# Attention and feed-forward on one core: two turned pairs of heads in one visit of TensorE, their last 64 query rows as float32 products in quarters of the array

## The chip, the cores and the metric

One Trainium2 chip, one core of it. The metric is the device time of one execution in microseconds (us), the median of several runs. The engines are named as in the profile: PE (TensorE, matrix products), PEld (its weight loads), DVE (VectorE), ACT (ScalarE), POOL (GpSimd), SP (SyncE, which issues most DMA transfers).

## The reference, cut to what matters

```python
B, H, S, D = 8, 8, 576, 64                # q, k, v: (B, H, S, D); f: (B, H, S)
scores = q @ k.T / sqrt(D)                # per batch and head
cum = cumsum(log(clip(f, 1e-4, 1)))
scores = where(above the diagonal, -1e9, scores + cum[:, None] - cum[None, :])
attn = softmax(scores)                    # rows, less their maximum
x = (attn @ v), heads side by side        # (4608, 512)
h = x @ w_in                              # (4608, 2048)
g = max(h, 0) + alpha * min(h, 0)
out = g @ w_out                           # (4608, 512)
```

Inputs and outputs are float32 (the two weight matrices arrive as float64 words and are rebuilt on the chip).

## The kernel before, in words

The work is 32 pairs of heads (n = 0 to 31, four pairs a batch), then a first feed-forward product in 9 blocks of 512 tokens (`ffn1(b)`, 192 products of 128x128 by 128x512 each), then a second one in 18 units of 256 tokens (`ffn2(u)`). The order is not written out: every operation is handed to a planner (`Plan.run`) with an engine, an estimated duration, a key and the buffers that it needs, and the planner puts each engine's operations in a fixed order. The key is a due time plus a number from the table `SHIFT` (one for each step letter and pair). An operation with `glue` may be chosen although PE would have to wait for it up to that many us; `need=(ring, k)` holds an operation back until k buffers of a ring are free or their last readers have been placed. Engines then run their lists in order, and wait on semaphores where data or buffers are late.

PSUM has 8 banks, shared by rings: `rS` (scores, tails and, from batch 1 on, the values' results), `rH` (blocks of `ffn1`, two banks are kept for it), `rT` (transposes).

Pairs 8 to 31 are "turned": their rows of attention are transposed by DVE and DMA, not by PE. For a turned pair n, `attention(n)` makes these steps:

- `load_n`: q and k of both heads (one tile `rqk`, two of them) come in; ACT and POOL split them into high and low float32r parts Qh, Ql, Kh, Kl (ring `rQ`, two sets); tile 0's q and k are copied as they are to a small tile `qk`, since the first 128 query rows are done as one float32 product. The decay goes to Z (128 by 2 by 1280, ring `rZ`, two) and Zt.
- `visit`: PE makes, in one go, the values of an earlier pair (`values`, products of 128 rows by 64 columns, both heads side by side) and then the scores of this pair: tiles 0 and 1 in one bank for each head, tile 2, tile 3; six banks. Each score is three float32r products (Qh Kh, Qh Kl, Ql Kh); the two heads lie in the two halves of the array's rows (64 by 128).
- `tail`: the last 64 query rows of both heads as one product of 128 by 128. For this the host lays q out with blocks of zeros (640 columns in place of 576). Three float32r products for 256 and three for 320 key columns, in two banks. The planner puts them anywhere after the visit, or before it.
- `tile` and `red` in `tail`: DVE takes each bank, adds the decay, finds the row's minimum (L830, L680) and writes to `bE`, a single buffer of 3136 columns for a whole pair; ACT takes the exponential in place (`expo`, L637). When all nine parts are done, DVE transposes `bE` in four pieces (L846) and 16 DMA transfers lay them out for `values`. Until then the next turned pair can't write to `bE`, and its banks stay full.
- `quotients` and `rest`: the sums' reciprocals go through DRAM; `rest` scales the values' result and splits it for `ffn1`, into a ring `rx` of seven buffers, of which a block of `ffn1` holds four until its last product.

`ffn1` fills the time between the visits, in pieces of six products. Each of its banks is emptied by ACT (L1027) and then DVE (L1029).

Of the kernel before, what the change touches and what calls it, by code (L numbers as in the profile page):

```python
# [18 lines left out]
NP = H // 2  # L19
# [25 lines left out]
LAG = 2000  # L45
PJ = (2, 4, 6)
# [8 lines left out]
SHIFT = {('L', 0): 9.4, ('D', 0): 2.2, ('Z', 0): 60.6, ('A', 0): 2.2, ('T', 0): -0.3, ('V', 0): -13.3, ('Q', 0): 36.2, ('X', 0): -10.8, ('L', 1): 26.8, ('D', 1): 1.4, ('Z', 1): -27.5, ('A', 1): 47.1, ('T', 1): 17.0, ('V', 1): 48.8, ('X', 1): 122.0, ('L', 2): 28.7, ('D', 2): 45.5, ('Z', 2): 10.6, ('A', 2): 54.0, ('T', 2): 1.8, ('V', 2): 58.1, ('Q', 2): -44.8, ('X', 2): 24.9, ('L', 3): 15.8, ('D', 3): -69.7, ('Z', 3): 0.9, ('A', 3): 165.1, ('T', 3): -84.7, ('Q', 3): 0.7, ('D', 4): -10.7, ('Z', 4): 63.2, ('A', 4): 13.0, ('T', 4): 4.2, ('V', 3): 35.9, ('Q', 4): 132.1, ('X', 3): -15.3, ('L', 5): 81.7, ('D', 5): -4.2, ('Z', 5): -0.4, ('A', 5): 21.2, ('T', 5): -65.7, ('V', 4): 1.3, ('Q', 5): -3.4, ('X', 4): 18.4, ('L', 6): 69.8, ('D', 6): 30.4, ('A', 6): 173.3, ('T', 6): 64.2, ('V', 5): 16.9, ('L', 7): 15.0, ('D', 7): -6.8, ('Z', 7): -95.9, ('A', 7): 218.4, ('T', 7): 47.3, ('V', 6): -17.7, ('V', 7): -37.7, ('Q', 7): -7.0, ('X', 5): -14.8, ('X', 6): -7.2, ('W', 0): 14.3, ('W', 1): 178.8, ('W', 2): 130.1, ('W', 3): -7.0, ('W', 4): 29.0, ('W', 5): 13.1, ('W', 6): 131.9, ('W', 7): -0.1, ('W', 8): -24.7, ('W', 9): 48.7, ('W', 10): -21.0, ('W', 11): -226.7, ('W', 12): -27.8, ('W', 13): 9.3, ('W', 14): 110.8, ('W', 15): 19.8, ('L', 8): -132.0, ('D', 8): -70.2, ('Z', 8): -11.8, ('S', 8): 10.0, ('A', 8): 59.0, ('L', 9): 6.4, ('D', 9): -6.1, ('Z', 9): 32.3, ('S', 9): -81.3, ('A', 9): -1.9, ('Q', 9): -96.4, ('X', 7): 3.1, ('L', 10): 50.1, ('Z', 10): 7.2, ('S', 10): 75.8, ('A', 10): -14.4, ('V', 8): -29.5, ('L', 11): 6.9, ('Z', 11): 41.4, ('S', 11): -6.8, ('A', 11): -68.7, ('V', 9): 12.9, ('Q', 11): 10.9, ('X', 8): 37.3, ('X', 9): 119.6, ('L', 12): 6.3, ('Z', 12): -18.6, ('S', 12): 23.7, ('A', 12): -9.9, ('V', 10): -2.9, ('L', 13): 2.6, ('Z', 13): -3.7, ('S', 13): 27.4, ('A', 13): 27.1, ('V', 11): -0.8, ('Q', 13): -134.7, ('X', 10): 5.7, ('X', 11): 5.8, ('L', 14): 1.6, ('Z', 14): 459.3, ('S', 14): -32.6, ('A', 14): -10.4, ('V', 12): 1.0, ('L', 15): 34.3, ('Z', 15): 17.4, ('S', 15): 96.4, ('A', 15): -40.5, ('V', 13): -69.9, ('Q', 15): -38.3, ('X', 13): 4.3, ('L', 16): 2.7, ('Z', 16): -198.9, ('S', 16): -187.7, ('A', 16): 154.9, ('V', 14): -18.6, ('L', 17): -9.2, ('Z', 17): 0.6, ('S', 17): 49.4, ('A', 17): -109.5, ('Q', 17): -229.2, ('X', 14): 26.2, ('X', 15): -29.2, ('L', 18): -40.0, ('Z', 18): -30.3, ('S', 18): 19.5, ('A', 18): -44.4, ('V', 16): 8.7, ('L', 19): -4.1, ('Z', 19): 16.8, ('S', 19): -29.0, ('A', 19): -99.9, ('V', 17): -19.8, ('Q', 19): -113.9, ('X', 16): 4.8, ('X', 17): -2.5, ('L', 20): -18.2, ('Z', 20): -4.1, ('S', 20): 3.5, ('A', 20): -15.6, ('V', 18): -13.2, ('L', 21): 24.2, ('Z', 21): -5.1, ('S', 21): 30.9, ('A', 21): 1.5, ('V', 19): -12.3, ('Q', 21): -6.5, ('X', 18): -66.7, ('X', 19): 21.5, ('L', 22): -197.2, ('Z', 22): -25.6, ('S', 22): -118.4, ('A', 22): 52.2, ('V', 20): 46.3, ('L', 23): 3.6, ('Z', 23): 49.0, ('S', 23): 3.0, ('A', 23): -4.3, ('V', 21): 106.1, ('Q', 23): -43.7, ('X', 20): 27.7, ('X', 21): -18.4, ('L', 24): -6.9, ('Z', 24): 91.0, ('S', 24): 17.4, ('A', 24): 103.3, ('V', 22): -23.4, ('L', 25): -7.9, ('Z', 25): 14.7, ('S', 25): -51.9, ('A', 25): 20.7, ('V', 23): 21.8, ('Q', 25): 14.2, ('X', 22): 35.9, ('X', 23): -3.3, ('L', 26): -42.8, ('Z', 26): 29.2, ('S', 26): 11.4, ('A', 26): 78.5, ('V', 24): 156.6, ('L', 27): -38.3, ('Z', 27): 1.9, ('S', 27): 40.9, ('A', 27): 0.5, ('Q', 27): 2.0, ('X', 24): -6.8, ('X', 25): 12.5, ('L', 28): -1.5, ('Z', 28): -21.7, ('S', 28): 28.1, ('A', 28): -23.8, ('V', 26): 13.8, ('L', 29): 6.3, ('Z', 29): -5.4, ('S', 29): -109.1, ('A', 29): -4.1, ('V', 27): -32.8, ('Q', 29): -0.6, ('X', 26): -3.0, ('X', 27): -14.3, ('L', 30): -20.4, ('Z', 30): 3.6, ('S', 30): 13.5, ('A', 30): 40.4, ('V', 28): 9.6, ('L', 31): -7.6, ('Z', 31): -99.0, ('S', 31): 13.9, ('A', 31): -1.5, ('V', 29): 16.7, ('V', 31): 16.3, ('V', 30): -2.0, ('Q', 31): -48.0, ('X', 28): -51.3, ('X', 29): -14.3, ('X', 30): -12.2, ('X', 31): -79.3}  # L55
# [167 lines left out]
def attention_moe(  # L223
# [54 lines left out]
    def split_set(i):  # L278
        return (sp.tile([128, QW - 128], F32R, name=f"Qh{i}"), sp.tile([128, QW - 128], F32R, name=f"Ql{i}"),
                sp.tile([128, S], F32R, name=f"Kh{i}"), sp.tile([128, S], F32R, name=f"Kl{i}"), sp.tile([128, 256], F32, name=f"qk0{i}"))  # L280
# [3 lines left out]
    rqk = Ring(Store(qkt))  # L284
    rZ = Ring(Store([(sp.tile([128, 2, ZW], F32, name=f"Z{i}"), sp.tile([128, S], F32, name=f"Zt{i}")) for i in range(2)]))
# [198 lines left out]
    def load_n(n, held):  # L484
# [5 lines left out]
        q_, k_ = (lambda: bqk.t[:, 0:QW]), (lambda: bqk.t[:, QW : QW + S])  # L490
# [3 lines left out]
        if n < NQ:  # L494
            l_qk = [op("SP", 450, lambda c0=c0, c1=c1: sy.dma_start(bqk.t[:, c0:c1], qk[p][:, c0:c1]), kq, dq, [bqk], kb=(c1 - c0) / 2)
                    for c0, c1 in ((0, QW), (QW, QW + S))]
        else:
            l_qk = [op("SP", 500, lambda: sy.dma_start(bqk.t[:, 0:1024].rearrange("p (c n) -> p c n", c=2), qk1[b, p].rearrange("c p n -> p c n")), kq, dq, [bqk], kb=400),
                    op("SP", 500, lambda: sy.dma_start(bqk.t[:, 1024:], qk2[b, p]), kq, dq, [bqk], kb=96)]
# [74 lines left out]
        else:  # L574
            tz = [op("SP", 400, lambda h=h, c8_=c8_: sy.dma_start(Zt()[64 * h : 64 * h + 64], c8_[bh + h : bh + h + 1].broadcast_to([64, S])), kl + 1, o_, [bZ], kb=147) for h in range(2)]
# [9 lines left out]
        q0, k0_ = (lambda: bQ.t[4][:, 0:128]), (lambda: bQ.t[4][:, 128:256])  # L585
        out += [op("ACT", c_acs(128), lambda: ac.activation(q0(), q_()[:, 0:128], AF.Copy), kc, l_qk[:1], [bqk, bQ]),
# [12 lines left out]

    waiting, behind, later_x, quick_ops, value_ops, turn_ops = [], [], [], [], [], []  # L600

    def attention(n):

        b, p = divmod(n, NP)
        k0 = NS * n
# [788 lines left out]
```

## Time and profile before

| | |
|---|---|
| median of 3 runs | 990.89 us (990.79 to 997.57) |
| the profiled execution: time, span of the core | 990.63 us, 988.8 us |
| PE busy, PEld busy | 982.2 us (99%), 827.5 us (84%) |
| DVE, ACT, POOL busy | 830.7 us (84%), 614.4 us (62%), 375.5 us (38%) |
| granted TensorE clock | 1.000 over the span |
| transferred | 191.68 MB, 194 GB/s mean |

An engine's busy time is the union of its instructions' spans. PE's instructions overlap, so what one costs is read from the starts of the instructions after it, not from its own length.

### The profile page before, as it was taken

To read this page: it belongs to the slowest core of one execution; us is meant where nothing else is said; L and a number is where in the kernel's file an instruction comes from. 1 tells how busy PE (TensorE), PEld (TensorE's weight loads), DVE (VectorE), ACT (ScalarE), POOL (GpSimd) and SP (SyncE) were. 2 spreads that over 40 slices of the span, in tenths; PEclk is the share of its full clock that TensorE was granted. 3 is DMA by queue.
4 is the path that set the end of the run, shared out by engine and by line. 5 is a ranking of instruction groups with operands and counts; after the bars stand their busy time and mean duration, and the time that the engine had idled before them with its cause. 6 is when DMAs were issued, how large, how long until landed. Compare 5 with 4: busy or idle time off the path is not lost.

```text
span 988.8 us, 20133 instructions
## 1 busy us (share of the span) xinstructions
PE 982.2 (99%) x6935; PEld 827.5 (84%) x6935; DVE 830.7 (84%) x1585; ACT 614.4 (62%) x1399; POOL 375.5 (38%) x652
## 2 busy tenths in 40 slices
PE   9999999999999999999999999999999999999998
PEld 5777788888888888888888888999888988898898
DVE  6899988878787778779637988789999999999995
ACT  7888887878677686767635655645444543544352
POOL 5465976888868797777350000000000000000000
PEclk9999999999999999999999999999999999999999
DMA  7977768888888798796757655553444344334521
GB/s 216 260 215 259 251 217 247 254 246 262 247 251 255 224 261 249 219 267 200 215 180 237 203 172 200 174 170 107 149 128 149 107 149 155 122 107 149 169 67 43
DMA packets 133876, 191.68 MB, mean 194 GB/s; under 512 B 22647, under 2 KB 84590, under 8 KB 133774
## 3 DMA queue, kind: packets, MB, share of 16 engines
q1 hardware_dynamic: 128878, 175.73, 57.2%
q0 software_dynamic: 4608, 14.46, 5.3%
q8 instruction: 55, 0.90, 0.4%
q14 instruction: 47, 0.39, 0.1%
q10 hardware_dynamic: 288, 0.20, 0.1%
HBM read 102.95 MB, written 48.67 MB: 153 GB/s over the span
## 4 chain that ended last, share of the span: by engine, by line
PE 96%; DVE 2%; issue 1%; DMA 0%; ACT 0%; DVEq 0%; ACTq 0%
PE bank L381 93%; PE bank L651 2%; PE bank L444 0%; DMA wr<-in_w_in_dram 0%; DVE xs L939 0%; DVE hs L371 0%; DVE big L830 0%; PE bank L729 0%; PE bank L479 0%; DVE hs L1316 0%; DVE big L646 0%; DVE hs L368 0%; DVE wr L371 0%; DVE hs L367 0%; DVE wr L368 0%
## 5 line engine op out<-in xcount | busy, mean ns | idle before, releaser
L381 PE MATMUL bank<-xx,wi 128*128 128x512 f32 x1728 | 407.2, 392 | 0.0
L381 PEld LDWEIGHTS bank<-xx,wi 128*128 128x128 f32 x1728 | 320.4, 188 | 69.6 <-issue 3.0
L637 ACT ACTIVATE big<-big,st 128x384 f32<-128x384 f32 (+4 forms) x272 | 157.7, 582 | 25.8 <-DVE st L830 24.2
L1029 DVE SCALAR_TENSOR_TENSOR hs<-bank,sa,hs 128x512 f32<-128x512 f32 x116 | 86.5, 745 | 54.0 <-ACT hs L1027 52.5
L1027 ACT ACTIVATE hs<-bank,ab 128x512 f32<-128x512 f32 x116 | 79.7, 687 | 70.6 <-PE bank L381 69.0
L830 DVE CUSTOM_DVE_ANT_0 big<-bank,Z 128x384 f32<-128x384 f32 (+1 forms) x220 | 93.0, 480 | 34.2 <-PE bank L381 27.7
L1268 ACT ACTIVATE xx<-gj 128x1792 fp32r<-128x1792 f32 x37 | 62.4, 1701 | 95.0 <-DVE gj L1261 57.3
L381 PE MATMUL bank<-wot,xx 128*128 128x256 f32 (+1 forms) x734 | 120.6, 323 | 0.0
L381 PE MATMUL bank<-wi,xx 128*128 128x256 f32 (+1 forms) x734 | 120.6, 323 | 0.0
L381 PEld LDWEIGHTS bank<-wi,xx 128*128 128x128 f32 x734 | 106.8, 189 | 12.2
L381 PEld LDWEIGHTS bank<-wot,xx 128*128 128x128 f32 x734 | 106.8, 189 | 12.2
L846 DVE STREAM_TRANSPOSE big<-big 128x768 f32<-128x768 f32 x96 | 90.3, 959 | 8.5 <-ACT big L637 8.5
L543 POOL TENSOR_TENSOR Z<-Z,tri 128x128 f32<-128x128 f32 x192 | 79.8, 444 | 34.3 <-DVE Z L513 30.7
L1269 DVE TENSOR_TENSOR xx<-gj,xx 128x1792 fp32r<-128x1792 f32 x37 | 74.4, 2018 | 2.5 <-ACT xx L1268 2.5
L943 POOL TENSOR_TENSOR xx<-xs,xx 128x256 fp32r<-128x256 f32 x64 | 49.0, 781 | 43.2 <-ACT xx L941 42.7
L381 PEld LDWEIGHTS bank<-big,vr 128*64 128x64 f32 x1168 | 53.7, 137 | 9.1 <-issue 5.5
L381 PE MATMUL bank<-wi,gh 128*128 128x256 f32 (+1 forms) x370 | 60.9, 322 | 0.0
L381 PE MATMUL bank<-wot,gh 128*128 128x256 f32 (+1 forms) x370 | 60.9, 322 | 0.0
L381 PE MATMUL bank<-big,vr 128*64 128x128 f32 (+1 forms) x1168 | 59.7, 260 | 0.0
L381 PEld LDWEIGHTS bank<-wot,gh 128*128 128x128 f32 x370 | 53.9, 189 | 6.0
L381 PEld LDWEIGHTS bank<-wi,gh 128*128 128x128 f32 x370 | 53.9, 189 | 6.0
L1298 ACT ACTIVATE hs<-bank 128x256 f32<-128x256 f32 x102 | 36.5, 384 | 24.9 <-PE bank L381 24.6
(164 smaller groups left out, 1585.6 us busy)
## 6 DMA issues: line engine op xcount, KB each, us to landing
hd<-hs SPq DMA_DIRECT2D x144, 256.0 KB
gj<-hd SPq DMA_DIRECT2D x50, 512.0 KB
rqk<-in_qk_dram SPq DMA_DIRECT2D x28, 512.0 KB
wx<-hd SPq DMA_DIRECT2D x22, 512.0 KB
vr<-in_vv_dram SPq DMA_DIRECT2D x32, 320.0 KB
wr<-in_w_in_dram SPq DMA_DIRECT2D x16, 512.0 KB
wx<-in_w_out_dram SPq DMA_DIRECT2D x16, 512.0 KB
out_dram<-hs SPq DMA_DIRECT2D x30, 256.0 KB
```

The costliest lines, as they stand in the source:

```text
L381: pe.matmul(o, lhsT, rhs, start=start, stop=stop)
L543: ms.append(op("POOL", c_po(128), lambda to=to, i=i, zd=zd: po.tensor_tensor(to()[:, :, -1:], zd()[:, :, i : i + 1], tk(), ALU.add), kc + ...
L637: ex = op("ACT", c_exp(w), lambda: ac.activation(at(bt.t), at(bt.t), AF.Exp, bias=lo()[:, col : col + 1], scale=-1.0, accum_out=su()[:, co ...
L651: pe.transpose(t[:, c : c + 128], src[:, 128 * j : 128 * j + 128], ident)
L830: ve.tensor_tensor_reduce(out=o if turned else blk(o), in0=blk(bS.t[:, c0 : c0 + w]), in1=in1(), scale=-0.125, scalar=3.0e38, op0=ALU.add, ...
L846: ve.transpose(part(b_[:, 0 : 768 if k < 3 else MW]), part(bE.t[:, c0 : c0 + (768 if k < 3 else MW)]))
L943: xl = op("POOL", c_po(256), lambda r=r, t0=t0: po.tensor_tensor(bx.t[:, 1, t0 : t0 + 256], bxs[r].t[:, 0:256], bx.t[:, 0, t0 : t0 + 256]. ...
L1027: cp = op("ACT", c_act(512), lambda bh=bh, bs=bs, fc=fc: ac.activation(bs.t, bh.t, AF.Relu, scale=ab[:, fc : fc + 1]), -1000, [last, o_sg] ...
L1029: cp = op("DVE", c_dve(512), lambda bh=bh, bs=bs, fc=fc: ve.scalar_tensor_tensor(bs.t, bh.t, sa[:, fc : fc + 1], bs.t, ALU.mult, ALU.add), ...
L1268: hi = op("ACT", c_acs(896 * GW), lambda w=w, bgh=bgh: ac.activation(bgh.t[:, 0], w(), AF.Copy), key, [o2], [bj, bgh])
L1269: lo = op("DVE", c_dve(896 * GW), lambda w=w, bgh=bgh: tt(bgh.t[:, 1], w(), bgh.t[:, 0].bitcast(F32), ALU.subtract), key + 0.1, [hi], [bj, ...
L1298: side = op("ACT", c_act(256), lambda m=m, slot=slot: ac.activation(bs.t[:, slot], bo[m].t[:, 256:512], AF.Copy), kd, [last], [bo[m], bs])
```

## The change

Turned pairs are taken two at a time by `couple(n)`: `attention` becomes a generator `steps` that stops after its loads and again after its scores.

- PE's visit for a couple is now: tails of both pairs against the first 256 keys, tails of both against the other 320 keys, scores of pair n, values of two earlier pairs, scores of pair n+1. All are keyed -3000 with glue 1.5; the first tail operation also needs five banks of `rS` (`NEED`).
- A tail is now one float32 product of 64 by 64 for each head, with no zeros: head h of pair n in row half h and column half h, of pair n+1 in row half h and column half 1-h (`swap`), so that the four products of a step lie in the four quarters of the array. The odd pair's tail rows therefore come out with the heads exchanged; its Zt, its sums' columns, its side of `bri` and its tail blocks in `values` are exchanged to match.
- The odd pair's tail can't go to `bE` yet; DVE writes it to a new tile `tt`, from where `expo` takes it to `bE`.
- Tile 0's float32 product and the tails read q and k from `rqk` itself: the two copies to `qk` are gone, Qh and Ql have 384 columns (512 before), and `rqk` is held until the pair's scores are done. For turned pairs q arrives with 576 columns (640 before).
- `later_x` keeps three pairs back (two before), and the whole table `SHIFT` is another.

```diff
-        for hi, lo, raw, z, w, ld in ((Qh, Ql, q_, 128, QW, l_qk[:1]), (Kh, Kl, k_, 0, S, l_qk)):
+        for hi, lo, raw, z, w, ld in ((Qh, Ql, q_, 128, 512, l_qk[:1]), (Kh, Kl, k_, 0, S, l_qk)):
...
-        held.append(bQ)
+        held += [bQ, bqk]
...
+    def couple(n):
+
+        pair = steps(n), steps(n + 1)
+        got = [next(g) for g in pair]
+        vals = [behind.pop(0) for _ in range(min(2, len(behind) - 1))]
+        go = sum([d() for _, d in vals], []) + got[0][0] + got[1][0]
+        for g, (c0, c1) in enumerate(TC):
+            plan.at("A", n)
+            bS = [Buf(rS) for _ in range(2)]
+
+            def tails(bS=bS, g=g):
+                for (_, _, quarter, _), b_ in zip(got, bS):
+                    quarter(g, b_.t)
+
+            s = op("PE", c_m4(c1 - c0) + (20 if g else 170), tails, -3000, go, bS + got[0][1] + got[1][1], glue=1.5, need=None if g else (rS, NEED))
+            for (_, _, _, lowest), b_ in zip(got, bS):
+                lowest(g, s, b_)
+            go = [s]
+        run = [pair[0].send(go)]
+        for f_, d in vals:
+            vb, vp, vd, done = f_()
+            run.append(op("PE", ns_v[0] + 400, vp, -3000, [run[-1]], vb, glue=1.5))
+            value_ops.append(run[-1])
+            done(run[-1])
+        pair[1].send([run[-1]])
...
+        def quarter(g, t):
+
+            q, k = terms[3]
+            for h in range(2):
+                r, o, (c0, c1) = slice(64 * h, 64 * h + 64), 64 * (h ^ swap), TC[g]
+                mm(t[o : o + 64, : c1 - c0], q(512, S)[r], k()[r, c0:c1], True, True)
+
+        def lowest(g, s, bS):
+
+            plan.at("A", n)
+            c0, c1 = TC[g]
+            low.append(op("DVE", c_dve(c1 - c0) + 60, lambda: ve.tensor_tensor_reduce(
+                out=aside.t[:, c0:c1] if swap else tail_at(bE.t)[:, c0 // 64 : c1 // 64], in0=cut(bS.t[:, : c1 - c0]), in1=cut(bZ.t[1][:, c0:c1]), scale=-0.125, scalar=lo()[:, 9:10] if g else 3.0e38,
+                op0=ALU.add, op1=ALU.min, accum_out=lo()[:, 4:5] if g else lo()[:, 9:10]), k0 - 1 + 0.6 * g, [s, rt] + low, [bS, aside if swap else bE, bst, bZ]))
...
-        def visit(st):
+        def visit(st, go):
 
             plan.at("A", n)
-            after = behind.pop(0) if len(behind) > 1 else None
-            go = rdy
-            if after:
-                vb, vp, vd, done = after()
-                a = op("PE", ns_v + 400, vp, st, rdy + vd, vb, need=(rS, len(vb[:2]) + 4))
-                value_ops.append(a)
-                done(a)
-                plan.at("A", n)
-                go = [a]
...
+        if turned:
+            where = visit(k0, (yield rdy, held, quarter, lowest))
+            yield s_0[-1]
+            plan.at("A", n)
...
-    for n in range(NX[0], B * NP):
-        attention(n)
+    for n in range(NX[0], B * NP, 2):
+        couple(n)
```

## Rows read from the trace of the kernel before

**Rows 1.** The chain that ended last, its final piece: start us, us, engine and line.

```profile
498.06 483.88 PE bank L381 x2864
```

**Rows 2.** Busy time by stretch: stretch and its length, then each engine, clock, DMA.

```profile
127.00:250.00 123.00, 123.00 (x997) 101.45 (x997) 100.89 (x253) 94.89 (x276) 99.83 (x183) 1.00 0.82 242
250.00:375.00 125.00, 125.00 (x1065) 104.42 (x1063) 98.37 (x247) 92.25 (x268) 100.11 (x178) 1.00 0.84 249
375.00:501.00 126.00, 126.00 (x1082) 104.74 (x1076) 96.71 (x246) 87.98 (x255) 84.96 (x152) 1.00 0.79 227
501.00:660.00 159.00, 159.00 (x845) 135.87 (x846) 121.92 (x180) 87.31 (x122) 8.19 (x13) 1.00 0.57 191
660.00:820.00 160.00, 160.00 (x979) 142.51 (x979) 152.71 (x191) 71.71 (x88) 0.00 (x0) 1.00 0.42 135
```

**Rows 3.** PE's timeline, 285 to 295 us: start us, us, then what ran, count.

```profile
285.27 0.39 PE L381 MATMUL bank<-Kh,Qh 128*128 128x256 f32 x1
285.49 0.28 PE L381 MATMUL bank<-Kl,Qh 128*128 128x256 f32 x1
285.61 0.28 PE L381 MATMUL bank<-Kh,Ql 128*128 128x256 f32 x1
...
286.17 8.35 PE L381 MATMUL bank<-xx,wi 128*128 128x512 f32 x36
294.45 0.33 PE L381 MATMUL bank<-wr,vr 128*64 128x128 f32 x2
```

**Rows 4.** PE's timeline, 323 to 334 us: one visit, and a tail later.

```profile
322.78 2.99 PE L381 MATMUL bank<-wr,vr 128*64 128x128 f32 x60
325.70 0.39 PE L381 MATMUL bank<-Kh,Qh 64*128 64x256 f32 x2
...
326.29 0.42 PE L381 MATMUL bank<-Kh,Qh 64*128 64x384 f32 x2
...
326.90 0.39 PE L381 MATMUL bank<-Kh,Qh 64*128 64x512 f32 x2
...
327.69 5.74 PE L381 MATMUL bank<-xx,wi 128*128 128x512 f32 x24
333.27 0.28 PE L381 MATMUL bank<-Kh,Qh 128*128 128x256 f32 x1
...
333.62 0.31 PE L381 MATMUL bank<-Kh,Qh 128*128 128x320 f32 x1
...
334.06 0.39 PE L381 MATMUL bank<-xx,wi 128*128 128x512 f32 x1
```

**Rows 5.** PE's timeline, 82 to 84 us: an early pair's tail, in float32.

```profile
82.65 0.60 PE L381 MATMUL bank<-rqk 128*128 128x256 f32 x2
83.09 0.49 PE L651 MATMUL bank<-ident,big 128*128 128x128 f32 x3
83.42 0.70 PE L381 MATMUL bank<-rqk 128*128 128x320 f32 x2
83.96 0.27 PE L729 MATMUL bank<-ident,st 128*9 128x128 f32 x1
```

**Rows 6.** DVE's timeline, 315 to 330 us: one pair's scores, tail and transposes.

```profile
315.29 0.29 DVE L830 CUSTOM_DVE_ANT_0 big<-bank,Z 128x128 f32<-128x128 f32 x1 [2.31 <-PE bank L381]
...
316.40 0.55 DVE L830 CUSTOM_DVE_ANT_0 big<-bank,Z 128x384 f32<-128x384 f32 x1
...
318.58 0.42 DVE L680 CUSTOM_DVE_ANT_0 big<-bank,Zt 128x256 f32<-128x256 f32 x1
...
319.18 0.55 DVE L680 CUSTOM_DVE_ANT_0 big<-bank,Zt,st 128x320 f32<-128x320 f32 x1 [0.17 <-DVE st L680]
...
320.89 0.75 DVE L1029 SCALAR_TENSOR_TENSOR hs<-bank,sa,hs 128x512 f32<-128x512 f32 x1
...
329.54 0.29 DVE L830 CUSTOM_DVE_ANT_0 big<-bank,Z 128x128 f32<-128x128 f32 x1 [0.17 <-DVE big L846]
```

**Rows 7.** Groups of 127 to 501 us, POOL: line, engine, operation, count, busy us, mean ns.

```profile
L595 POOL TENSOR_TENSOR Ql<-rqk,Qh 128x512 fp32r<-128x512 f32 x22 | 28.5, 1295 | 14.0 <-ACT Qh L590 13.7
```

**Rows 8.** The timelines of PE and of POOL around 212 us.

```profile
209.74 5.60 PE L381 MATMUL bank<-xx,wi 128*128 128x512 f32 x24
...
215.35 0.73 POOL L943 TENSOR_TENSOR xx<-xs,xx 128x256 fp32r<-128x256 f32 x1
```

More of the change, by code (lines that the diff above doesn't have):

```diff
@@ L489, in load_n @@
         bqk, bZ = Buf(rqk), Buf(rZ)
-        q_, k_ = (lambda: bqk.t[:, 0:QW]), (lambda: bqk.t[:, QW : QW + S])
+        late = n >= NX[0]
+        wq = S if late else QW
+        q_, k_ = (lambda: bqk.t[:, 0:wq]), (lambda: bqk.t[:, wq : wq + S])
+        side = n >= NX[0] and n % 2
         plan.at("L", n)
@@ L574, in load_n @@
         else:
[L575 removed]
+            tz = [op("SP", 400, lambda h=h, c8_=c8_: sy.dma_start(Zt()[64 * (h ^ side) : 64 * (h ^ side) + 64], c8_[bh + h : bh + h + 1].broadcast_to([64, S])), kl + 1, o_, [bZ], kb=147) for h in range(2)]
         plan.at("Z", n)
@@ L596, in load_n, with steps @@
                     lo()[:, a0 - z : a1 - z], raw()[:, a0:a1], hi()[:, a0 - z : a1 - z].bitcast(F32), ALU.subtract), kc, [o1], [bqk, bQ]))
-        held.append(bQ)
-        return out, rz, rt, bZ, [(lambda a, b, q=q: q()[:, a - 128 : b - 128], k) for q, k in ((Qh, Kh), (Qh, Kl), (Ql, Kh))] + [(lambda a, b: q0(), k0_)]
-    waiting, behind, later_x, quick_ops, value_ops, turn_ops = [], [], [], [], [], []
+        held += [bQ, bqk]
+        return out, rz, rt, bZ, [(lambda a, b, q=q: q()[:, a - 128 : b - 128], k) for q, k in ((Qh, Kh), (Qh, Kl), (Ql, Kh))] + [(lambda a, b: q_()[:, a:b], k_)]
+    waiting, behind, later_x, quick_ops, value_ops, turn_ops, ns_v = [], [], [], [], [], [], []
     def attention(n):
+        for _ in steps(n):
+            pass
+    def couple(n):
[20 more added lines that the diff above has]
+        pair[1].send([run[-1]])
+        for g in pair:
+            for _ in g:
+                pass
+    def steps(n):
         b, p = divmod(n, NP)
@@ L612, in attention @@
         turned = NX[0] <= n < NX[1]
+        swap = turned and n % 2
         plan.at("L", n)
@@ L665, in tail @@
             plan.at("A", n)
-            bt = bE if turned else Buf(re)
+            bt = Buf(re)
             prev = None
@@ L793, in stretch @@
             after = behind.pop() if tiles == (2,) and behind else None
-            vb, vp, vd, done = after() if after else ([], lambda: None, [], lambda o: None)
-            ns = 340 + sum(c_row(128 * i + 128, nt_) for i in tiles) + (ns_v if after else 0)
+            vb, vp, vd, done = after[0]() if after else ([], lambda: None, [], lambda o: None)
+            ns = 340 + sum(c_row(128 * i + 128, nt_) for i in tiles) + (ns_v[0] if after else 0)
             s = op("PE", ns, lambda: (prods(), vp()), st, rdy + vd, [x for y in bS for x in y] + held + vb)
@@ L951, in attention @@
         k_ = (0, 2, 6, 8) if n < NE else (0, 0.5, 2, 3) if turned else (0, 2, 8, 6)
-        bt = None
+        bt = where = None
+        if turned:
+            where = visit(k0, (yield rdy, held, quarter, lowest))
+            yield s_0[-1]
+            plan.at("A", n)
+        mate = waiting[-1] if n >= NV2 and n % 2 else None
+        bsu = mate[0] if mate else bst
+        if turned:
+            bt = bE
+            nt = expo(bE, S, 4, k0 - 0.4, low[1:], tail_at, (lambda: aside.t.rearrange("p (m c) -> p m c", c=64)) if swap else None, [aside] if swap else [])
         for tiles in ((0, 1), (2,), (3,)) if n < NE else ((2, 3, 0, 1),) if turned else ((0, 1, 3), (2,)):
-            where = visit(k0) if turned else stretch(tiles, -61 if n + tiles[0] == 0 else k0 + k_[tiles[0]])
+            where = where or stretch(tiles, -61 if n + tiles[0] == 0 else k0 + k_[tiles[0]])
             for i in tiles:
@@ L969, in values @@
                     lambda o: [done_v(r, bP[r])(o) for r in (1, 0)])
-        behind.append(values)
+        behind.append((values, v_deps))
         plan.at("V", n)
@@ L990, in attention @@
         elif not (n >= NV2 and n % 2 == 0):
-            keep = 2 if turned else 1
+            keep = 3 if n > NX[0] + 1 else 2 if turned else 1
             for f_ in later_x[:-keep]:
```

59 lines of the change are left out of this document (29 added, 30 removed).

## The prediction

> **What bounds the kernel now.** I read the chain of waits first. Its last piece is PE alone for 483.88 us [rows 1], and most of the chain before it is PE too. Then the busy time by stretch: PE is busy for all of 127 to 501 us, where the turned pairs run, and for all that follows up to 820 us, while POOL, DVE and ACT are busy for 67 to 82% of the first three stretches [rows 2]. So from 127 us on the time is the sum of PE's products. The timeline of PE must show whether that busy time has waits in it, since a busy PE may only be a full pipeline. It has nearly none: 36 products of `ffn1` take 8.28 us, 0.23 each, and the values after them start without a gap [rows 3]; the visits have one pattern throughout (values 2.92 us, scores 1.99, tail 0.80) [rows 4]. A us of PE taken out of this stretch comes off the end, if nothing else becomes late, and a us of waiting put in comes on top. Work saved on POOL, ACT or DMA is worth nothing by itself.
>
> **The sum, part by part.** It is made against the profiled execution, 990.63 us (span 988.8 and 1.83 around it); the median of the runs is 0.26 above it.
>
> *Tails removed.* Among products of `ffn1` a tail takes from 333.27 to 334.06 = 0.79 us, 0.35 for the step of 256 keys and 0.44 for that of 320 [rows 4]. There are 24 of them (a count over the timeline: 144 products, six a pair): 19.0 us.
>
> *Tails added.* The trace has no 64 by 64 product. What a float32 product costs by its columns is in the early pairs: two passes, 0.44 us for 256 columns and 0.54 for 320 [rows 5]. If the four quarters run at the same time, a couple costs 0.44 + 0.54 = 0.98, twelve couples 11.8 us. If they run two at a time it is 1.96 and 23.5 us, one by one 47 us. That is the disputed price. Nearest rows: the two heads of a score lie in halves of the rows, and three products of 512 columns for both take 0.79 us with the switch after them, where one such product of `ffn1` takes 0.23, so the heads overlap [rows 3, 4]. The two heads of the values lie in halves of the columns; 20 products of 128 and 10 of 64 columns would, at 0.11 us a pass by the 0.44 of 256 columns, take about 5.5 us in a row and take 2.92 [rows 4, 5], so they overlap too. Row halves and column halves each work, with different moving data in each; I take four at a time: saved 19.0 - 11.8 = 7.2 us.
>
> *Switches.* When the array goes from one division to another, the first product takes longer: 0.22 us in place of 0.12 for the tail right behind scores [rows 3], so about 0.10 a switch. Before, two pairs have six (into the values, into the scores, back to 128 by 128, twice); now there are five (tails, scores, values of two pairs together, scores, back). Saved 12 x 0.1 = 1.2 us.
>
> *Waits inside the longer visit.* This is the added cost, and nothing in the trace shows it, since before the values come first and give the banks time. Count from the first tail product, with six banks for the visit. PE: tails until 0.98, switch 0.1, scores of tiles 0 and 1 0.59, of tile 2 0.61, of tile 3 0.79 with the switch behind it [rows 4]; so tile 3 is reached at 2.3 and the values at 3.1 us. DVE: it starts some 0.3 after the first step's 0.44; the four tail parts take 0.35, 0.35, 0.48, 0.48 (a part is read from its start to the next one's, 0.61 for the widest), the four of tiles 0 and 1 together 1.11 (315.29 to 316.40) [rows 6]. So the tails' banks are free at 2.4 and those of tiles 0 and 1 at 3.5: a wait of 0.1 before tile 3 and 0.4 before the values, 0.5 a couple. It is less if a bank that `ffn1` has left is taken, or if a piece of `ffn1` is placed between (then two switches, 0.2); it is more if DVE has an `ffn1` bank to empty in between, 0.75 [rows 6]. Bounds 0 and 1.5 us a couple (two such banks); I take 0.3, near the count: +3.6 us.
>
> *Steps moved, at no cost.* The second pair's scores can't be emptied until the first pair's `bE` is transposed. Before it is the same: scores made from 325.70 were first read at 329.54 [rows 4, 6]. A pair holds `bE` for 14.3 us (315.29 to 329.54), a couple for 28.5, and a couple has 374/12 = 31 us; the cover is 2.7 us a couple, and if it goes, PE runs `ffn1` on two banks as it did then. The odd pair's tail goes through `tt` with the same DVE and ACT operations. POOL loses the copies to `qk` and a quarter of the Ql subtraction (0.3 of 1.3 us each [rows 7]), ACT as much: hidden work, worth nothing. `rqk` is held longer, so the next loads are issued later; behind them in SP's queue stand the stores of `ffn1` blocks and the layouts of `bE`. Loads and splits of a couple have the some 20 us between two visits. The first 127 us keep their operations; only the table reorders them: 0, with 3 us to either side. The second product follows PE and keeps its length.
>
> Sum: -7.2 - 1.2 + 3.6 = -4.8 us; 990.63 - 4.8 = 985.8, and 0.26 for the median: **986 us**.
>
> **Rivals.**
>
> *No waits and a better start.* If the banks are always free in time and the table takes 2 us out of the first 127: -8.4 - 2 = -10.4, **980.5**. For it: DVE is idle for a fifth of these stretches [rows 2], and before it hid every such wait. Against: the count above, with DVE at once on the tails, still gives 0.5.
>
> *Two quarters at a time.* 23.5 - 19.0 - 1.2 = +3.3; the slower tails give DVE time, so waits are 0 to 2 us more: **995**. For it: no row shows four. Against: both kinds of halves overlap in the rows above. The Trainium skill has a rule of this kind: TensorEngine Tiling (Array Packing), section Restrictions and Gotchas, says that different row tiles cannot access the same PSUM bank simultaneously, and here the two heads of one pair, in different row halves, write one bank. By that rule the heads of a pair would have to take turns, and the sum would be this one; no run here shows such a case, as the scores' heads have a bank each.
>
> *The visit waits for DVE (slower).* The place is the six banks between the tails and the values. If DVE is behind by two `ffn1` banks (2 x 0.75) when the tails come, each couple loses 1.5 us: -8.4 + 18 = +9.6, **1000**. It decides from 8.4/12 = 0.7 us a couple, not far above my 0.5. For it: DVE is 77 to 82% busy [rows 2], the tails are now first and in a burst, and nothing else on PE covers it once the visit has begun. Against: before, no visit shows a wait.
>
> *`ffn1` runs dry.* A block needs the values of four pairs. Values now come up to a pair later (those of pair 11 went with pair 13's visit, and go between the scores of 14 and 15). Before, block 2 began at 212.5 us, in the middle of the first of these rows, and the last piece of its input was written at 216.1 [rows 8], so there was nothing to spare; later blocks have more. One stall of up to 10 us, 5 taken: -4.8 + 5, **991**.
>
> **How the numbers follow.** Forecast (986, from 982 to 989.5 with waits of 0 to 0.6 a couple) 0.45; no waits 0.20; two at a time 0.10; DVE's waits 0.12; dry 0.13. The range holds the forecast, most of the better case, the dry one and two at a time, and leaves out the far half of the better case and DVE's: 979.5 to 997. Faster by over 1% means under 981.0, about what a measurement tells from no change: 0.14, from the better case. Slower by over 1%, over 1000.8: 0.07, half of DVE's case and quarters one by one. Within: 0.79.
>
> **What would show it.** In the trace after: 64 by 64 tail products that start four together and take about 1.0 us of PE a couple (two at a time: 2.0); DVE's tail parts running while PE is at the scores; a gap before the values of 0 to 0.5 us; PE's last turned stretch ending 5 us earlier, and the second product as long as before. I am wrong if the quarters wait for each other, if gaps in the visit exceed 0.7 us a couple, or if the first 127 us move by more than 3.

## The result, and the profile after

The changed kernel takes 1004.6 us (median of four runs, 1002.34 to 1010.89) beside 991.1 of the kernel before: ratio 1.0145, 95% interval 1.0117 to 1.0173. The forecast was 986.0, its range ended at 997. The profiled execution took 1002.34 us (span 1000.6, 11.8 longer than before).

**Where the loss lies.** The second product is as long as before. The chain's last piece now starts later and ends at 993.66 us, where it ended at 981.94 before [rows 1], and from the last product of `ffn1` to that end it is 350.1 us in both kernels. That last product (of block 8, where the turned stretch ends) starts at 643.56 us instead of 631.81, and the 126th product of `ffn1`, about where the turned pairs begin, at 118.81 instead of 117.69. So some 11 us are lost between 119 and 644 us.

```profile
515.24 478.42 PE bank L383 x2840
```

The windows that answer to [rows 2] show it: in the first three PE is no longer busy throughout, and there DVE, ACT and POOL are no busier than before, but for DVE in the first.

```profile
127.00:250.00 123.00, 120.03 (x957) 92.30 (x955) 103.23 (x270) 89.29 (x264) 88.22 (x162) 1.00 0.77 227
250.00:375.00 125.00, 123.87 (x990) 98.63 (x987) 90.41 (x220) 82.97 (x243) 90.09 (x163) 1.00 0.82 236
375.00:501.00 126.00, 122.90 (x1046) 97.01 (x1046) 88.66 (x226) 80.14 (x232) 78.79 (x141) 1.00 0.73 215
501.00:660.00 159.00, 159.00 (x906) 134.62 (x905) 121.25 (x193) 90.77 (x144) 19.71 (x29) 1.00 0.62 204
660.00:820.00 160.00, 160.00 (x998) 143.37 (x997) 152.76 (x192) 74.07 (x94) 0.00 (x0) 1.00 0.43 138
```

**The tails came out as forecast.** PE's timeline, the start of a visit (it answers to [rows 4]): the sixteen records of the quarters take from 177.91 to 179.04, 1.13 us with the switch into them. Eleven of the twelve visits have this length; one, at 412.59, takes 2.54, since `rqk` came late. A piece of six products of `ffn1` lies inside the visit, between two parts of a pair's scores; the last row is the values that follow.

```profile
177.12 0.86 PE L383 MATMUL bank<-xx,wi 128*128 128x512 f32 x3
177.91 1.20 PE L383 MATMUL bank<-rqk 64*64 64x256 f32 x16
179.04 0.39 PE L383 MATMUL bank<-Kh,Qh 64*128 64x256 f32 x2
...
179.82 1.65 PE L383 MATMUL bank<-xx,wi 128*128 128x512 f32 x6
181.40 0.45 PE L383 MATMUL bank<-Kh,Qh 64*128 64x384 f32 x2
...
182.83 1.42 PE L383 MATMUL bank<-wr,vr 128*64 128x128 f32 x22
```

**An account of PE.** I summed PE's time from each start to the next, by kind of product, from 119 us to the end of block 8 (for `ffn1`, what lies above 0.2275 us a product [rows 3]), and counted how often the array changes its division. The last two columns are experiments from further below.

```
us                  before  after  layouts_away  next_tuned
tails                20.68  14.98         13.57       13.57
values               72.93  71.43         71.42       71.88
scores               48.50  58.43         53.41       52.43
ffn1 above 0.2275     4.74  13.49         10.95        8.71
end of block 8      631.81 643.56        633.87      630.05
changes of division     79    103           103         106
```

Tails give 5.7 us back and values 1.5; scores and `ffn1` take 18.7 more. The products have not become slower. Part of it is the piece in the rows above: from 179.04 to 182.83 are 3.79 us, where a pair's scores alone take 1.99 [rows 4] and six products of `ffn1` 1.37, so putting the piece there costs 0.43. Of the 24 turned pairs 16 have their scores broken in this way, 2 before: 14 more, some 6 us. The rest is waits: runs of scores or of `ffn1` that are longer than the usual run of their kind by more than 0.1 us are so by 12.9 us together. The view of PE's waits (us in total, times, longest), empty for this stretch before, holds 6.8 us of them in all (it counts from the modelled end of a product) and names mostly DVE:

```profile
PE bank L383 <- POOL xx L982: 1.7, 2, 1.2
PE bank L777 <- DVE st L775: 1.4, 1, 1.4
PE bank L383 <- DVE hs L1078: 1.3, 5, 0.4
PE bank L383 <- DVE st L708: 1.1, 3, 0.6
```

**DVE stands idle ahead of the transposes.** The groups of DVE over the whole span, the transposes of `bE` before and after: busy time and mean hardly change, the idle time ahead of them goes from 8.5 to 65.6 us, and most of it ends with a layout transfer (`wr<-big`).

```profile
L846 DVE STREAM_TRANSPOSE big<-big 128x768 f32<-128x768 f32 x96 | 90.3, 959 | 8.5 <-ACT big L637 8.5
```

```profile
L885 DVE STREAM_TRANSPOSE big<-big 128x768 f32<-128x768 f32 x96 | 91.7, 968 | 65.6 <-DMA wr<-big 39.7 <-ACT big L671 13.1 <-DMA big<-big 5.8
```

One such stop, in three timelines of the kernel after. DVE (it answers to [rows 6]) is through with its work at 218.0 and stands for 4.79 us, though the scores of the visit's second pair are made from 219.91 on; it takes the first of them at 228.46, behind the transposes.

```profile
217.27 0.74 DVE L520 STREAM_TRANSPOSE Zt<-sel 128x576 f32<-128x576 f32 x1
222.79 0.98 DVE L885 STREAM_TRANSPOSE big<-big 128x768 f32<-128x768 f32 x1 [4.79 <-DMA wr<-big]
...
227.30 1.01 DVE L885 STREAM_TRANSPOSE big<-big 128x800 f32<-128x800 f32 x1 [0.60 <-DMA wr<-big]
228.46 0.29 DVE L869 CUSTOM_DVE_ANT_0 big<-bank,Z 128x128 f32<-128x128 f32 x1
```

SP: the layout transfers of the odd pair before begin only at 217.25,

```profile
217.25 7.70 SPq L893 DMA_DIRECT2D wr<-big  x10
225.00 1.45 SPq L651 DMA_DIRECT2D vr<-in_vv_dram  x2
```

and PE: they begin when the values that read the layout tile `wr` are done (214.22 to 217.04).

```profile
214.22 2.99 PE L383 MATMUL bank<-wr,vr 128*64 128x128 f32 x60
217.04 2.94 PE L383 MATMUL bank<-big,vr 128*64 128x128 f32 x60
219.91 0.39 PE L383 MATMUL bank<-Kh,Qh 64*128 64x256 f32 x2
...
225.78 1.89 PE L383 MATMUL bank<-xx,wi 128*128 128x512 f32 x7 [0.17 <-DVE hs L1078]
228.10 1.41 PE L383 MATMUL bank<-xx,wi 128*128 128x512 f32 x5 [0.43 <-POOL xx L982]
```

So this was the reading that went into the experiments, theory A: values, then the layout tile is free, then the layouts of a waiting pair, then the four small tiles that the transposes fill, then the transposes, then `bE`, then the second pair's scores. Theory B: nothing of this matters, the two pairs' nine parts each simply come to DVE in one burst. Theory C: the new table of due times is at fault, not the structure.

### The profile page after: what moved, and what is told of

Read it like the earlier page. It is cut to its first block, busy times and chain, and to the rows that moved or that the text cites. A ratio compares the mean times of both kernels' runs of the same rounds, so it can differ in the third digit from the quotient of the medians.

```text
span 1000.6 us, 20078 instructions
## 1 busy us (share of the span) xinstructions
PE 985.6 (98%) x6969; PEld 814.2 (81%) x6969; DVE 828.9 (83%) x1585; ACT 603.4 (60%) x1375; POOL 361.7 (36%) x628
## 4 chain that ended last, share of the span: by engine, by line
PE 74%; DMA 7%; DVE 6%; SPq 5%; ACT 4%; issue 2%; POOL 1%; DVEq 0%; ACTq 0%; POOLq 0%
PE bank L383 72%; SPq L893 4%; ACT big L671 2%; DMA big<-big 2%; DMA rqk<-in_qk_dram 2%; DMA hd<-hs 1%; PE bank L685 1%; DVE big L885 1%; DVE big L869 1%; DMA vr<-in_vv_dram 1%; DMA wr<-big 1%; DVE hs L1078 1%; DMA ri<-rd 1%; ACT hs L1076 0%; POOL Z L548 0%
## 5 line engine op out<-in xcount | busy, mean ns | idle before, releaser
L383 PE MATMUL bank<-xx,wi 128*128 128x512 f32 x1728 | 411.7, 394 | 3.5 <-POOL xx L982 1.7
L671 ACT ACTIVATE big<-big,st 128x384 f32<-128x384 f32 (+4 forms) x260 | 148.5, 574 | 19.0 <-DVE st L708 15.5
L885 DVE STREAM_TRANSPOSE big<-big 128x768 f32<-128x768 f32 x96 | 91.7, 968 | 65.6 <-DMA wr<-big 39.7
L383 PE MATMUL bank<-rqk 64*128 64x128 f32 (+6 forms) x448 | 58.4, 397 | 0.7 <-ACT big L681 0.3
```

The source lines that it names most:

```text
L383: pe.matmul(o, lhsT, rhs, start=start, stop=stop)
L671: ex = op("ACT", c_exp(w), lambda: ac.activation(at(bt.t), of() if of else at(bt.t), AF.Exp, bias=lo()[:, col : col + 1], scale=-1.0, accu ...
L885: ve.transpose(part(b_[:, 0 : 768 if k < 3 else MW]), part(bE.t[:, c0 : c0 + (768 if k < 3 else MW)]))
```

## The experiments

**Tables taken out (before_no_table, after_no_table).** Both kernels with all due times at their keys.

```diff
+SHIFT = {}
```

> The kernel before with an empty table SHIFT, to be read beside the changed kernel with an empty table. Theories of the 11 to 14 us lost by the change: (A) the chain of tiles: the values of two earlier pairs now come behind the first scores, back to back; the tile that the layouts of the previous odd pair write to is free only after them, DVE stands at its transposes until those layouts are through, and whatever is behind on DVE, the emptying of banks too, comes late for PE. (B) the burst: DVE is too busy with tails and scores of two pairs to give banks back in the visit. (C) the table: the code is as good as before or better, the new table orders it badly. A and B expect this one at 992 to 1000 and the changed one with an empty table at least 12 us above it; C expects the changed one with an empty table 4 to 8 us below it.

> The changed kernel with an empty table. A and B: at least 12 us above the kernel before with an empty table, 1008 to 1030, with DVE idle ahead of its transposes for 40 us or more by A. C: 4 to 8 us below it.

Measured: 996.25 (995.11 to 997.7) and 1036.25 (1030.91 to 1039.88), with 991.0 for the kernel before. Without tables the change costs 40 us; its table recovers 32, that of before 5. Theory C is out: the table hides a cost of the structure. The group of transposes grew as theory A wants:

```profile
L885 DVE STREAM_TRANSPOSE big<-big 128x768 f32<-128x768 f32 x96 | 91.8, 967 | 86.1 <-DMA wr<-big 76.2 <-ACT big L671 4.7 <-ACT Z L546 4.6
```

**Values first (values_early_no_table).** The changed kernel, empty table, the parts of a visit (made functions: T tails, A and B the two pairs' scores, V values) in the order values, tails, scores, values, scores.

```diff
+        for step in 'VTAVB':
+            {"T": T, "V": V, "A": lambda: S(0), "B": lambda: S(1)}[step]()
```

> The changed kernel with an empty table and another order in the visit: values of one earlier pair, tails, scores of n, values of the other earlier pair, scores of n+1. A: one layout tile is free before the scores, so DVE's idle time ahead of its transposes falls by half or more, and the time is at least 10 us under that of the changed kernel with an empty table. B: tails and scores are as much of a burst as before, within 3 us of it. C says nothing of two kernels with an empty table: within 3 us.

Measured: 1008.99 (1005.38 to 1010.16), 27 us below after_no_table, and 22.9 us idle ahead of the transposes.

**Layouts without a tile (layouts_away).** The changed kernel with its table and queues, but the sixteen layout transfers of a turned pair go to a scratch area in DRAM, and the values are made from zeros. No transfer waits for a layout tile, and the values wait for no layout.

```diff
-    bTT.t[32 * k : 32 * k + 32, MW * a : MW * a + w_], bm[k].t[32 * a : 32 * a + 32, 0:w_]), k0 + 8 + j / 100, [tn], [bm[k], bTT], kb=w_ / 8))
+    lay[n % 4, k, a, :, 0:w_], bm[k].t[32 * a : 32 * a + 32, 0:w_]), k0 + 8 + j / 100, [tn], [bm[k], bTT], kb=w_ / 8))
```

> The changed kernel with its table and the same order on every engine, but the 16 layout transfers of a turned pair go to a scratch in DRAM and not to the tile that the values read (the values of turned pairs are made from zeros: that part of the computation is left out). The transfers no longer wait for a tile to be free. A: DVE's idle time ahead of the transposes for DMA (45 us) is gone to under 10, PE's waits with it, 992 to 996. B and C: DVE is as busy and the order is the same, 1000 to 1005.

Measured: 993.31 (991.53 to 994.93), ratio 1.0022 to before: 11.3 us of the 13.5 are gone (9.6 of 11.7 by the profiled runs). The values take the same time in both kernels (71.43 and 71.42 in the account), so it is not their own wait for layouts that went. DVE's burst is the same here, so theory B is out.

```profile
L886 DVE STREAM_TRANSPOSE big<-big 128x768 f32<-128x768 f32 x96 | 90.1, 961 | 28.4 <-ACT big L672 14.9 <-DMA lay<-big 5.9 <-ACT xs L965 5.2
```

**Two quarters instead of four (halves).** The odd pair uses the same two quarters as the even one.

```diff
-        swap = turned and n % 2
+        odd, swap = turned and n % 2, 0
```

> The changed kernel, its table and its order of queues, but the odd pair of a visit uses the same two quarters of the array as the even pair instead of the two on the other diagonal, so that only two quarters can be at work at a time. If the 16 records of a visit's tails of 1.13 us are four quarters at work at once, they take about 2.0 us here, and the kernel is 9 to 12 us longer than the changed one (1012 to 1016 beside 1003 to 1005). If what the trace shows as four at a time is only how records are drawn, or PE would have waited anyway, the time moves by less than 3 us.

Measured: 1012.26 (1011.39 to 1015.39), 7.7 above the changed kernel, a little less than the 9 to 12 expected; the tails of a visit take 2.09 us in place of 1.13 (212.78 to 214.87), 25.14 in all for 14.98. Four quarters do run at once. Of the 10.2 us more, scores give 6.0 back (52.48 for 58.43, perhaps because DVE has more time, which is not shown), while `ffn1` takes 3.9 more.

```profile
212.78 2.16 PE L383 MATMUL bank<-rqk 64*64 64x256 f32 x16
214.87 0.39 PE L383 MATMUL bank<-Kh,Qh 64*128 64x256 f32 x2
```

**The price of a change of division (probe_whole, probe_quarter).** The changed kernel with one extra product of 64 columns ahead of every bank of `ffn1`, with the whole array (probe_whole) or with a quarter of it (probe_quarter, whose edit stands here).

```diff
+    if c == 0:
+        pe.matmul(bh.t[0:64, 0:64], wi[0:64, fc, 0, 0, 0:64], x[0:64, 0, 0:64], start=True, stop=True)
```

> The changed kernel with one more product ahead of every bank of ffn1: 64 columns, with the whole array as the ffn1 products (128x128), into the bank that the first true product then starts anew; it adds nothing to the result. It is the yardstick for the next run: some 0.04 to 0.07 us for each of 16 banks of a block, and no switch of the array's division. About 0.05 x 128 = 6 us to the end of block 8 by either theory, less where PE would have waited.

> The same extra product of 64 columns, but in a 64x64 quarter of the array, so that PE changes its division twice more for every bank of ffn1. Theory S (a change of division costs about 0.2 us, and the 24 more of them are 4 to 5 us of the loss): the stretch from the product ahead to the second true product is 0.3 to 0.45 us longer than in the run with the whole array, and the kernel 38 to 60 us longer than that run. The rival (0.1 us each, as the forecast had it): 0.2 us a bank, 25 us longer. If a change is free, the two runs agree.

Measured: 1013.99 and 1040.59 (one run each). Inside runs of `ffn1` the steps from the start of the product ahead of the extra one to that of the third behind it are 0.226, 0.029, 0.313 and 0.231 us with the whole array, and 0.318, 0.171, 0.338 and 0.227 with the quarter (medians of 99 and 100 places after 200 us): 0.255 more for going in and out, 0.13 a change. That is nearer to the forecast's 0.10 than to theory S's 0.2, and so are the 26.6 us between the two kernels (144 extra products, 252 more changes between 119 us and the end of block 8). But it is the price of a lone product of 64 columns. A piece of `ffn1` between scores is entered and left for 0.43, 0.2 a change, as theory S has it; why the two differ stays open. The price of the changed kernel's pieces is therefore read from the pieces themselves, some 6 us, and not from 24 times 0.13.

```profile
200.52 0.19 PE L1066 MATMUL bank<-xx,wi 128*128 128x64 f32 x1
200.55 2.77 PE L383 MATMUL bank<-xx,wi 128*128 128x512 f32 x11
```

```profile
199.84 0.19 PE L1066 MATMUL bank<-xx,wi 64*64 64x64 f32 x1
199.96 3.00 PE L383 MATMUL bank<-xx,wi 128*128 128x512 f32 x12
202.89 0.24 PE L1066 MATMUL bank<-xx,wi 64*64 64x64 f32 x1
```

**Not holding PE (pieces_out), and tables for the order with values first (early_tuned, early_tuned_b, early_slack).** All from values_early_no_table: every part of a visit with glue 0.3 (0.5 in early_tuned_b), then tables, and in early_slack slower transfers in the planner too. In early_tuned_b `quotients` of turned pairs are also due 20 us later.

```diff
-                s = op("PE", (170 if g == 0 else 0) + c_row(w_, nt_), lambda part=part: rows_of_scores(part), -3000, got, bS[g] + held, glue=1.5)
+                s = op("PE", (170 if g == 0 else 0) + c_row(w_, nt_), lambda part=part: rows_of_scores(part), -3000, got, bS[g] + held, glue=0.3)
```

> The kernel of values_early_no_table (order values, tails, scores, values, scores; empty table) with one thing changed: the planner holds PE for the next part of a visit for 0.3 us instead of 1.5 us before it plays a piece of ffn1 first... that is, a part that is not ready within 0.3 us of PE's last product does not take PE from ffn1 work that is ready. The chain through the layout tiles is the same as in values_early_no_table, so theory A says nothing else than 1005 to 1009 unless fewer waits follow; theory S counts the changes of division: it was 115 there, and for each change fewer or more the time should go by 0.2 us. If PE's waits ahead of parts of visits (DVE not done with the piece before) were the rest of the loss, the time falls by 5 us or more, to 1000 to 1004, with no fewer changes.

> The order values, tails, scores, values, scores (as in pieces_out) with a table of due times found for that order. Theory A (the values come too late for the layout tiles; the rest is order and queues): with the values first and a table that takes out the 5 us that the empty table loses before 127 us and the loads that arrive late for ACT, 990 to 1000, below the changed kernel; the idle time of DVE ahead of the transposes stays under 30 us. Theory C' (two pairs in one visit cost time whatever the order of the parts): it stays at 1002 to 1010 like the changed kernel. At its best it meets the kernel before (991), since the tails are 7 us shorter and the changes of division and x that comes late take 3 to 7 back.

> The same order with another table, found by itself, and with 0.5 in place of 0.3 us that the planner holds PE for the next part of a visit. It tells how much of the result hangs on one table: within 4 us of early_tuned if the order decides, farther apart if the table does.

> The same order again, but the planner reckons with slower transfers (0.6 us more to begin and to end, 180 in place of 220 KB a us), so that it puts what waits for layouts and loads later in each queue, and its table was found with these. If waits in DVE's and ACT's queues for transfers that come later than planned are what is left of the loss, PE's waits over 0.25 us fall under 6 us (12.5 in pieces_out) and the time is 990 to 998. If the slower plan only moves work, it is as early_tuned or longer.

Measured: 1012.09 (1010.7 to 1013.71), 1005.84 (1004.12 to 1007.6), 1001.81 (1000.37 to 1004.98) and 1016.1 (1014.42 to 1018.84). For pieces_out 1000 to 1009 was expected, and theory A had promised 990 to 1000 for early_tuned; both missed. early_slack came out as its rival had it, longer than early_tuned. The values' place alone doesn't take the loss out, and a plan with slower transfers is worse.

**The same without the tile (early_away).** early_tuned with the edit of layouts_away.

> early_tuned with the layout transfers of turned pairs going to a scratch area in DRAM, as in layouts_away: the values are made from zeros, and no transfer waits for a layout tile. What is left of the chain in early_tuned is the difference. Theory A says under 4 us, since the values come first there (in the changed kernel it was 11 us). If the values' place made no difference to the chain, it is 8 us or more.

Measured: 992.87 (991.35 to 999.66), 13 us below early_tuned. So the chain was still there in early_tuned, against "under 4 us", though DVE's idle time ahead of the transposes was only 20.0 us in it: the wait had moved to another queue. One stop shows how. In SP's timeline of early_tuned the five layouts are issued at 217.66, right behind the values that free the tile (their products end at 217.54), and the load of q and k, later in the same queue, at 228.35;

```profile
217.66 3.30 SPq L904 DMA_DIRECT2D wr<-big  x5
...
227.08 1.17 SPq L904 DMA_DIRECT2D wr<-big  x2
228.35 0.54 SPq L503 DMA_DIRECT2D rqk<-in_qk_dram  x1
```

in early_away they are issued at 214.42 and 223.52.

```profile
214.42 2.19 SPq L905 DMA_DIRECT2D lay<-big  x5
...
223.52 0.40 SPq L504 DMA_DIRECT2D rqk<-in_qk_dram  x1
```

The next two rows are ACT's and PE's, both in early_tuned. ACT stands for the load, with a bank of `ffn1` behind it in its queue; DVE waits for ACT with the same bank, and PE for DVE.

```profile
232.75 0.52 ACT L591 ACTIVATE Qh<-rqk 128x384 fp32r<-128x384 f32 x1 [4.96 <-DMA rqk<-in_qk_dram]
```

```profile
234.69 1.65 PE L383 MATMUL bank<-xx,wi 128*128 128x512 f32 x3 [3.13 <-DVE hs L1089]
```

That led to the code. A visit of pairs n and n+1 makes the values of n-3 and n-2, and leaves those of n-1 (`len(behind) - 1`). There are two layout tiles, so pair n+1 needs that of n-1, which is read only in the next visit. In the kernel before, a visit of pair n makes the values of n-2 and frees at once the tile that n itself needs.

**Values a couple earlier (next_empty).** The changed kernel and the order of its visit, with an empty table; only which values a visit makes is changed, and each values part waits for its own layouts.

```diff
-        vals = [behind.pop(0) for _ in range(min(2, len(behind) - 1))]
-        go = sum([d() for _, d in vals], []) + got[0][0] + got[1][0]
+        vals = [behind.pop(0) for _ in range(min(2, len(behind)))]
+        go = got[0][0] + got[1][0]
...
-            run.append(op("PE", ns_v[0] + 400, vp, -3000, [run[-1]], vb, glue=1.5))
+            run.append(op("PE", ns_v[0] + 400, vp, -3000, vd + [run[-1]], vb, glue=1.5))
```

> The changed kernel with an empty table and the order of its visit (tails, scores, values, values, scores), but a visit of pairs n and n+1 makes the values of n-2 and n-1 in place of n-3 and n-2; each values part waits for its own layouts instead of the whole visit for both. It is compared with after_no_table (1036). Theory A2 (the odd pair's values come a couple late, so its layout tile is free only after the next visit, and the odd pair after it can't be laid out before): DVE's idle time ahead of the transposes falls from 86 to under 30 us and the time by 25 us or more, to 1000 to 1012. The rival (the place of the values within the visit, or two pairs in a burst, is what costs): 1025 to 1036, as values_early_no_table was 1009 by its order alone.

Measured: 1002.93 (1002.09 to 1005.22), 33 us below after_no_table, and the sign of theory A2 (the odd pair's values come a couple too late), DVE's idle time ahead of the transposes:

```profile
L885 DVE STREAM_TRANSPOSE big<-big 128x768 f32<-128x768 f32 x96 | 89.2, 954 | 5.4 <-ACT big L671 5.4
```

**Shorter holds, and the second values behind (next_half, next_behind).** next_empty with glue 0.5 for the parts of a visit; and that with the second values last, where `quotients` of turned pairs are also due 20 us later.

> next_empty with the planner holding PE for the next part of a visit for 0.5 us in place of 1.5. By theory A2 with PE's waits ahead of late parts as the second term: 4 to 10 us below next_empty, 994 to 1003, with more pieces of ffn1 inside visits (0.25 us for each that is entered and left). If being held costs nothing, within 3 us of next_empty.

> next_half with the second values after the scores of the second pair (tails, scores, values, scores, values). The values of n-1 then have 2 us more for their layouts, and its layout tile is free 1 us later. By theory A2 the same as next_half within 4 us, since either place is well ahead of the next need of the tile; if the place within the visit decides, farther apart.

Measured: 997.5 (995.64 to 998.56) and 1004.97 (1002.11 to 1005.97). The first agrees with A2. The second doesn't agree with "the same within 4 us": it is 7.5 longer, and PE waits 2.49 us for an `ffn1` bank once (until 209.03). With two things changed it does not tell which of them costs, and I have not followed that further. The kernel before without its table takes 996.25, so here the change costs no more than the scatter of the runs.

**Tables for it (next_tuned, next_tuned_a, next_tuned_b).** next_half with three tables.

> next_half with a table of due times found for it, begun from the changed kernel's entries for the first eight pairs and the weights. next_half loses 5 us before the 126th product of ffn1 against the changed kernel, and has 118 changes of division against 79 in the kernel before. By theory A2 and S: 997.5 less 4 to 6 for the start and 1 to 2 for fewer changes, 989 to 993, the same as the kernel before or a little below. The rival (an order that hangs on the table as early_tuned did, where tables took 3 to 10 us out of 1012): 993 to 998.

> next_half with another table. 989 to 994 if the order decides; over 996 if a table that wasn't made for these queues' real lengths undoes it.

> next_half with a third table. 989 to 994 if the order decides; over 996 if a table that wasn't made for these queues' real lengths undoes it.

Measured: 991.22 (988.23 to 997.92, ratio 1.0014, 0.9996 to 1.0031), 997.53 (994.85 to 998.87) and 990.46 (988.27 to 993.04, ratio 0.9995, 0.9985 to 1.0005). Two of three meet the kernel before, none beats it; next_tuned_a shows that a table still can undo the order.

## Why the prediction was wrong

**What bounds.** Right: the loss is PE's time in the turned stretch, most of it waiting where it had not waited.

**Tails.** Right: -7.2 us forecast; 20.68 less 13.57 is 7.1, in layouts_away and next_tuned (the changed kernel has 1.4 more from its one late visit). Four at a time was the right choice, and halves shows what two cost. The page TensorEngine Tiling (Array Packing) of the Trainium skill, section Restrictions and Gotchas, which says that different row tiles can't access one PSUM bank simultaneously, is not borne out here: the two heads of a pair, in different row halves, write the two partition halves of one bank and overlap: by [rows 5] four float32 records of the same columns take 0.98 us together, and all sixteen take 1.13. In halves, with two quarters in use, they take 2.09; heads that took turns would need some 3.9 there (an estimate, 4 x 0.98).

**Switches.** The term was -1.2 us from six to five per two pairs; there are 103 instead of 79 from 119 us to the end of block 8, as pieces of `ffn1` are put inside the visits. The text allowed for such a piece, at 0.2 us. It costs 0.43 and comes in 16 of 24 pairs: +5.8 us, what is left of scores and `ffn1` in layouts_away (11.1 us more than before) without their waits. Count and price were both too low: 7.0 us off.

**Waits inside the visit.** Forecast +3.6, 0.3 in every couple. Without the chain (layouts_away) it is 5.3, 1.7 above the term, but in three places, all before 157 us: 1.2 in the scores of the first visit's second pair, 3.3 in the run of `ffn1` behind it, 0.9 in the scores of the second visit. From there on no run of scores or `ffn1` is over 0.1 us longer than usual: the pieces lie where the waits were forecast. So the size came near by luck. The largest of the three is at the input of `ffn1`, which the rival "`ffn1` runs dry" had named:

```profile
PE bank L384 <- ACT xx L981: 1.6, 1, 1.6
PE bank L384 <- POOL xx L983: 0.7, 1, 0.7
```

**Steps moved, at no cost.** This is the step that failed, with 11.3 us of the 18.6 between forecast and result. It reckoned `bE` alone and gave it a cover of 2.7 us a couple. The cycle has more members: the transposes need the small tiles, these the layout transfers, these a layout tile, and that the values of two pairs earlier. The text even noted that values come up to a pair later, and asked of it only whether `ffn1` would run dry, not what else the values set free. Of SP's queue it named what stands behind the loads; in early_tuned the load stands behind the layouts, and that is how the same chain reaches ACT and PE in the stop that was followed.

**First 127 us, second product.** Right: 1.1 us later at the 126th product, and 350.1 us from the last product of `ffn1` to the chain's end on PE in both kernels.

Added up: 986.0 + 11.3 (tile) + 7.0 (switches) + 1.7 (waits) - 1.5 (values, not forecast) is 1004.5. The terms are read from the same account as the loss, so the sum has to come near. Of the rivals "the visit waits for DVE" came nearest in time (1000), but the place was another: DVE was not behind, it stood.

**What the change can give.** With the values a couple earlier and a table for it the kernel is where it was. next_tuned's account says why: 7.1 us of tails and 1.0 of values are saved, and 7.9 given back in scores and `ffn1`. Only 1.3 of these are waits (one run of scores, 318.6 to 321.8, has nearly all); the other 6.6 are pieces of `ffn1` inside the visits, again in 16 of 24 pairs. The view of PE's waits for the stretch has one row:

```profile
PE bank L383 <- ACT xs L964: 0.7, 1, 0.7
```

An order that leaves the visits whole without new waits was not found, and a third layout tile was not tried.

## What to carry to other kernels

When steps are batched, list every buffer that a batched step sets free, not only those it needs, and count in batches how much later each comes: with two buffers and work done in pairs, a step that lags by one unit before lags by a whole batch. A table of due times can hide such a cycle (32 of 40 us here), so compare structures with their tables taken out. Price what is put between two steps by its own rows: a probe of another shape had it too cheap here (0.13 a change for 0.2). When an experiment shortens a wait and the time stays, look for the same wait in another queue before giving up the cause.

## What was not expected of the hardware

PE's waits cost more than their length. Windows of early_tuned: from 418 to 421 us PE is busy for 1.08 of 3 us; then the granted clock is 0.51, so nearly all at the lower level (1.2 GHz), for the 7 us that follow, and full again from 428. At 234 to 240 us the same follows the wait of 3.13 us above. The timed runs of this kernel go from 1004.12 at a mean clock of 1.000 to 1007.6 at 0.991, so that in the slowest the clock is some 3 us of the loss. The empty tables have it too: 0.990 over the span of after_no_table, 0.998 of before_no_table and 0.997 of next_empty. From 220 to 230 us after_no_table has PE busy for 4.08 of 10 us and the clock at 0.71. So part of the 40 us and of the 33 us above is clock.

```profile
410.00:418.00 8.00, 8.00 (x94) 6.26 (x92) 6.09 (x10) 7.97 (x25) 7.65 (x16) 1.00 0.69 222
418.00:421.00 3.00, 1.08 (x15) 0.75 (x11) 3.00 (x6) 0.70 (x3) 2.98 (x6) 1.00 0.55 184
421.00:428.00 7.00, 6.55 (x28) 4.34 (x30) 4.48 (x24) 4.33 (x15) 2.23 (x5) 0.51 0.91 228
428.00:434.00 6.00, 6.00 (x82) 5.20 (x79) 5.81 (x9) 4.89 (x14) 3.36 (x7) 1.00 0.77 236
```

The changed kernel's profiled run, with waits up to 1.4 us in the view above, kept the full clock (1.000), but its longest timed run (1010.89) had 0.995, while the kernel before has 0.999 to 1.000 in the thirteen runs beside early_tuned. next_tuned scatters as much, from 988.23 at 0.999 to 997.92 at 0.994, though the longest wait in its profiled run's view is 0.7 us. None of these longer runs was traced, so what the clock fell after in them is not known.
